# Attention scores of two heads: one matmul over a zero-padded key block, or one matmul per head on half of TensorE's rows

## The chip, the cores and the metric

The kernel runs on one core of one Trainium2 chip. The metric is the device time of one execution in microseconds. Three executions of the kernel before took 631.2, 630.66 and 631.3 us; their median is 631.2 us.

## What is computed

Attention with pooled keys and values, then a channel mix. The shapes are batch 8, 8 heads, 576 positions, head size 64, model width 512, hidden width 1024, all in float32.

```python
k_p = k.reshape(B, H, Sp, pool, D).mean(axis=3)      # 8 positions -> 1: 72 keys
v_p = v.reshape(B, H, Sp, pool, D).mean(axis=3)
scores = scale * np.matmul(q, k_p.transpose(0, 1, 3, 2))
attn = softmax(scores)                               # over the 72 keys
x = (attn @ v_p), heads side by side                 # 4608 positions x 512
xk = mu_k * x + (1.0 - mu_k) * x_prev                # x_prev: the position before
xr = mu_r * x + (1.0 - mu_r) * x_prev
k = np.maximum(xk @ w_k, 0.0)
out = sigmoid(xr @ w_r) * (k * k @ w_v)
```

## The kernel before

The 4608 positions (8 batches of 576) are cut into 36 tiles of 128, and the tiles into chunks of 128, 256 and then eleven times 384 positions. A batch is four and a half tiles long, so tiles 4, 13, 22 and 31 hold the end of one batch and the start of the next, 64 positions each. They are called two-part tiles here; the other tiles have one part.

For each tile the kernel makes scores (`part`, line 719), a softmax over the 72 keys (lines 753 to 796), transposes of the probabilities (`transposed`, line 833, and `transposed_rest`, lines 878 and 888), and for each chunk the product with the values (`attended`, line 931), the mix with the position before (`joined`, line 985), and the three large products of the channel mix: `hidden` (line 1029), `gate` (line 1078) and `mixed` (line 1111). From the third chunk on these large products have float32r operands, split into a high and a low part, three matmuls for each product.

**The scores before.** Heads are taken in four pairs. The query tile `qs` holds a pair's two heads on its 128 partitions: the 64 elements of the first head on partitions 0 to 63, those of the second on 64 to 127. The keys of a batch lie in `kbd` (two of them, for even and odd batches), for each pair 128 partitions by 144 columns: columns 0 to 71 hold the first head's keys on partitions 0 to 63, columns 72 to 143 the second head's on partitions 64 to 127, and the other two quarters are zeros, cleared once. One float32 matmul of 128 rows, 128 weight columns (the queries) and 144 moving columns (the keys) thus gives the scores of both heads (line 729). A tile takes four of them, and a two-part tile eight, each with 64 of the queries as weights. TensorE runs a float32 matmul of this kernel as two passes, each with a weight load of its own, so the profile shows 8 records of matmuls for a tile and 16 for a two-part tile. The scores of pairs 0 and 1 go to the first PSUM bank of `sc`, those of pairs 2 and 3 to the second.

**The softmax.** VectorE takes the maximum of each head's 72 scores (line 753) and subtracts it (line 770, from `sc` to `e`), ScalarE takes the exponential (line 776), VectorE sums (line 778) and inverts (lines 781, 785), and GpSimd or VectorE multiplies (lines 791, 796). There is one `sc`, so the next tile's scores wait for line 770 of this one.

**What sets the order.** Every step is a Python generator with a due time. The class `Order` simulates the engines with a table of durations and writes the instructions of all five engines in the order that its simulation gives. For the scores of a tile it reckons with 1.0 us of TensorE (1.14 for a two-part tile); the change leaves these two figures as they are.

Of the kernel before, what the change touches and what calls it, by code (L numbers as in the profile page):

```python
# [12 lines left out]
ALU = mybir.AluOpType  # L13
AX = mybir.AxisListType
PSUM = bass.MemoryType.PSUM

P = 128
B, H, S, D = 8, 8, 576, 64
POOL = 8
KEYS = S // POOL  # L20
KM = 64
KR = KEYS - KM
NPAIR = H // 2
# [35 lines left out]
LOW_BY = {"k": "gvgvvvgv", "r": "gvgv", "v": "gvvggvgv"}  # L59
BY_HEAD = ((0, 1),)  # L60

BESIDE = (1,)
SQUARED_ON_ACT = (8, 0)
COPIES_ON_ACT = ()
# [166 lines left out]
def dve(n, lock=True):  # L231
    return "dve", 0.067 + n / 960, lock


def act(n, func=None):
    return "act", 0.1 + n / 1200, False, func
# [11 lines left out]
def attention_then_channel_mix(  # L248
# [13 lines left out]
    nc = tc.nc  # L262
# [26 lines left out]
    kbd = [const.tile([P, NPAIR, 2 * KEYS], F32, name=f"kbd{i}") for i in range(2)]  # L289
# [61 lines left out]
    for tag, n in EARLY:  # L351
        t = sb.tile([P, n, 2 * POOL * KEYS], F32, name=f"early_{tag}", tag=tag)
# [16 lines left out]
    def stretches(at, n):  # L369
        o, parts = 0, []  # L370
        while o < n:
            b, s = divmod(at + o, S)
            k = min(S - s, n - o)
            parts.append((b, s, k, o))
            o += k
        return parts

    units = [stretches(a, n) for a, n in zip(starts, CHUNKS)]
    tiles = [
        (c, o, stretches(a + o, P)) for c, (a, n) in enumerate(zip(starts, CHUNKS)) for o in range(0, n, P)  # L380
    ]
# [194 lines left out]
    def sums(st, cols, eng):  # L576

        raw, v = st
        if eng == "t":
            bank, o = yield from summed(v, cols)  # L580
            done_with("stage", raw)
            return "mm", bank, o
        for n in (4, 2, 1):
            yield (dve if eng == "v" else pool)(2 * n * cols)
            halve(nc.vector if eng == "v" else nc.gpsimd, v, cols, n)
        return "stage", raw, v[:, :, :cols]
# [29 lines left out]
    def values(b, p):  # L616
# [3 lines left out]
        if not b:  # L620
            yield need(*[("scored", i) for i in BESIDE])
        kind, raw, o = yield from sums(held.pop(("v", 2 * b + p)), D, SUM_BY.get(f"v{2 * b + p}", "g"))
# [66 lines left out]
    def softmax(i):  # L689

        parts = tiles[i][2]
        if i:
            yield need(("scoring", i - 1))
        yield need(("q", i), *[("keys", b, p) for b, *_ in parts for p in range(1 if i in HALVED else 2)])
        pair = None
        if i in BESIDE:
            pair = [(yield take("mm")), (yield take("mm"))]
            sc = None
            halves = [t.rearrange("p (a n) -> p a n", a=1) for t in pair]
        else:  # L700
            sc = yield take("sc")
            halves = [sc[:, a:a + 1] for a in range(2)]
        held["halves", i] = sc, pair, halves
        if i in HALVED:
            for kind in ("mx", "e", "sm", "px", "pm"):
                held[kind, i] = yield take(kind)
        order.make(("scoring", i))
        if i in HALVED:
            yield from part(i, 0, 1)
        else:  # L710
            yield from part(i, 0, 2)

    def shared(kind, i):
        if (kind, i) not in held:
            held[kind, i] = yield take(kind)
        return held[kind, i]

    def part(i, a0, a1):
        parts, na = tiles[i][2], a1 - a0
        mine = slice(a0, a1)  # L720
        yield need(("scoring", i))
        sc, pair, halves = held["halves", i]
        yield need(*[("keys", b, p) for b, *_ in parts for p in range(a0, a1)])
        qs = held["q", i]
        yield "pe", (1.0 if len(parts) == 1 else 1.14) * na / 2, False
        for g in range(2 * a0, 2 * a1):
            k = (g % 2) * 2 * KEYS
            for b, _, n, o in parts:
                nc.tensor.matmul(  # L729
                    out=halves[g // 2][o:o + n, 0, k:k + 2 * KEYS],  # L730
                    lhsT=qs[:, g, o:o + n], rhs=kbd[b % 2][:, g, :], start=True, stop=True,
                )
        order.make(("scores", i, a0))

        def emptied():
            order.make(("emptied", i, a0))
            if pair:
                for a in range(a0, a1):
                    order.give("mm", pair[a])

        if na == 1:
            svs = [halves[a0]]
        else:
            svs = [sc] if pair is None else halves
        svs = [t[:, :, :4 * KEYS].rearrange("p a (h k) -> p a h k", k=KEYS) for t in svs]
        n = 8 * KEYS // 2 * na
        mx = (yield from shared("mx", i))
        e = (yield from shared("e", i))
        sm = (yield from shared("sm", i))
        at = [mine] if len(svs) == 1 else [slice(0, 1), slice(1, 2)]  # L750
        for sv, o in zip(svs, at):
            yield dve(n // len(svs), False)
            nc.vector.tensor_reduce(out=mx[:, o], in_=sv, axis=AX.X, op=ALU.max)
        if (i, a0) in BY_HEAD:
            yield "dve", 0.11, True
            nc.vector.tensor_scalar(
                out=mx[:, mine], in0=mx[:, mine], scalar1=-scale, scalar2=None, op0=ALU.mult
            )
            yield "act", 1.2 * na, False, "exp"
            for a in range(a0, a1):  # L760
                for h in range(4):
                    nc.scalar.activation(
                        out=e[:, a, h], in_=halves[a][:, 0, h * KEYS:(h + 1) * KEYS], func=AF.Exp, scale=scale,
                        bias=mx[:, a, h], accum_out=sm[:, a, h],
                    )
            emptied()
        else:
            for sv, o in zip(svs, at):
                yield dve(n // len(svs), False)
                nc.vector.tensor_tensor(  # L770
                    out=e[:, o], in0=sv, in1=mx[:, o].broadcast_to([P, (2 if na == 2 and len(svs) == 1 else 1), 4, KEYS]),
                    op=ALU.subtract,
                )
            emptied()
            yield act(n, "exp")
            nc.scalar.activation(out=e[:, mine], in_=e[:, mine], func=AF.Exp, scale=scale)  # L776
            yield dve(n, False)
            nc.vector.tensor_reduce(out=sm[:, mine], in_=e[:, mine], axis=AX.X, op=ALU.add)
        order.make(("maxima", i, a0))
        yield "dve", 0.12, True  # L780
        nc.vector.tensor_scalar(
            out=sm[:, mine], in0=sm[:, mine], scalar1=1e-9, scalar2=float(POOL), op0=ALU.add, op1=ALU.mult
        )
        yield "dve", 0.195, False
        nc.vector.reciprocal(out=sm[:, mine], in_=sm[:, mine])  # L785
        px = (yield from shared("px", i))
        pm = (yield from shared("pm", i))
        v = NORM_BY.get(i, "g") == "v"
        eng = nc.vector if v else nc.gpsimd
        yield dve(4 * KR * na) if v else ("pool", 0.12 + 0.06 * na, True)  # L790
        eng.tensor_tensor(  # L791
            out=px[:, mine], in0=e[:, mine, :, KM:], in1=sm[:, mine].broadcast_to([P, na, 4, KR]), op=ALU.mult
        )
        order.make(("px", i, a0))
        yield dve(4 * KM * na) if v else ("pool", 0.05 + 0.47 * na, True)
        eng.tensor_tensor(
            out=pm[:, mine], in0=e[:, mine, :, :KM], in1=sm[:, mine].broadcast_to([P, na, 4, KM]), op=ALU.mult
        )
        order.make(("pm", i, a0))
# [353 lines left out]
    for i in range(NT):  # L1153
        spare = SPARE if tiles[i][0] > 1 else 0.0
        order.add(tile_due[i], softmax(i), spare)
        order.add(tile_due[i], gathered(i))
        if i in HALVED:
            order.add(tile_due[i] + 0.05, part(i, 1, 2), spare)
        order.add(tile_due[i] + 0.1, transposed(i), spare)
        order.add(tile_due[i] + 0.1, transposed_rest(i), spare)  # L1160
# [63 lines left out]
```

## Time and profile before

| | |
|---|---|
| median of three runs | 631.2 us (630.66 to 631.3) |
| the profiled execution | 631.48 us, of which the profile's span is 629.7 us |
| TensorE matmuls | busy 622.3 us, 99% of the span, 3355 records |
| TensorE weight loads | busy 548.0 us, 87% |
| VectorE, ScalarE, GpSimd | 63%, 56%, 34% |
| granted TensorE clock | 1.0 of full speed |

The profile is one execution. PE is TensorE's matmul row and PEld its weight loads, which run beside matmuls; DVE is VectorE, ACT ScalarE, POOL GpSimd, SP SyncE, which issues the loads and stores. A matmul's record is longer than the time that it holds the array, since matmuls are pipelined: what one costs is read from the distance between the starts of neighbours. A timeline row gives the start and length in microseconds of a run of like instructions and their number (x8); 128*64 means 128 rows and 64 weight columns, 128x144 the partitions and moving columns of the result's rows. Idle time and what ended it stand in brackets.

### The profile page before, as it was taken

What the parts mean: (1) busy time and instruction counts of PE and PEld (TensorE: products, weight loads), DVE (VectorE), ACT (ScalarE), POOL (GpSimd) and SP (SyncE); (2) the same over time, 40 slices, a digit from 0 to 9 for tenths busy, and PEclk for the clock granted to TensorE, in tenths of its full rate; (3) what the DMA queues carried; (4) which work ended last, traced back from release to release, by engine and by line L of the source; (5) the groups of instructions that cost most, each with busy time, mean ns of one, the idle gap of its engine ahead of it and who ended that gap; (6) DMA issues with size and microseconds to landing.
All of it is one profiled execution on the core that took longest, in us unless ns stands there. A gap on an engine that the chain in (4) does not pass through costs nothing.

```text
span 629.7 us, 9238 instructions
## 1 busy us (share of the span) xinstructions
PE 622.3 (99%) x3355; PEld 548.0 (87%) x3355; DVE 394.2 (63%) x792; ACT 350.9 (56%) x755; POOL 215.3 (34%) x338
## 2 busy tenths in 40 slices
PE   8999999999999999999999999999999999999997
PEld 8986559988989989989988988988988988988986
DVE  5999969968824645937635665759854655553411
ACT  3776866766525855556645555545655556454320
POOL 1422287448015128128125019217415106104000
PEclk9999999999999999999999999999999999999999
DMA  8696332051330012411011051032100100000001
GB/s 309 233 364 217 108 128 89 18 179 52 125 110 34 0 34 82 137 34 51 0 34 52 25 193 45 6 137 78 55 34 34 33 18 35 17 1 18 33 1 50
DMA packets 19005, 50.45 MB, mean 80 GB/s; under 512 B 2256, under 2 KB 2512, under 8 KB 18960
## 3 DMA queue, kind: packets, MB, share of 16 engines
q1 hardware_dynamic: 18960, 49.87, 22.6%
q8 instruction: 26, 0.43, 0.3%
q14 instruction: 19, 0.16, 0.1%
HBM read 40.43 MB, written 9.44 MB: 79 GB/s over the span
## 4 chain that ended last, share of the span: by engine, by line
PE 88%; ACT 3%; DVE 3%; POOL 3%; DMA 2%; issue 1%; SPq 0%; POOLq 0%; ACTq 0%; DVEq 0%
PE mm L1029 30%; PE mm L1111 29%; PE mm L1078 16%; PE bank L931 5%; PE sc L729 4%; PE bank L833 2%; DMA got_wr<-in_w_r 1%; DMA stage<-in_kT 1%; PE bank L424 1%; PE bank L434 1%; PE bank L888 1%; POOL stage L559 1%; ACT e L776 0%; ACT tmp L522 0%; DVE got_wk L527 0%
## 5 line engine op out<-in xcount | busy, mean ns | idle before, releaser
L1029 PE MATMUL mm<-xkh,w_k 128*128 128x384 f32 x704 | 180.9, 337 | 0.0
L1111 PE MATMUL mm<-w_v,sh 128*128 128x512 f32 x528 | 173.3, 394 | 0.0
L1029 PEld LDWEIGHTS mm<-xkh,w_k 128*128 128x128 f32 x704 | 126.0, 188 | 1.0 <-issue 0.6
L1029 PE MATMUL mm<-xkl,w_k 128*128 128x384 f32 x352 | 117.7, 335 | 0.0
L1111 PEld LDWEIGHTS mm<-w_v,sh 128*128 128x128 f32 x528 | 99.3, 188 | 19.4
L1111 PE MATMUL mm<-w_v,sl 128*128 128x512 f32 x264 | 103.0, 390 | 0.0
L791 POOL TENSOR_TENSOR px<-e,sm 128x64 f32<-128x64 f32 (+1 forms) x33 | 10.9, 331 | 225.7 <-DVE sm L785 219.9
L1078 PE MATMUL mm<-w_r,xrh 128*128 128x512 f32 x264 | 86.0, 397 | 0.0
L985 DVE SCALAR_TENSOR_TENSOR xm<-bank,given,t 128x384 f32<-128x384 f32 x88 | 50.6, 612 | 40.2 <-POOL t L959 23.0
L944 ACT ACTIVATE t<-bank,om_sb 128x384 f32<-128x384 f32 (+1 forms) x96 | 47.9, 573 | 50.0 <-PE bank L931 49.8
L1052 ACT CAST sh<-rk 128x384 fp32r<-128x384 f32 x88 | 45.0, 513 | 50.2 <-DVE rk L1046 50.0
L1121 DVE TENSOR_TENSOR rs<-mm,rs 128x512 f32<-128x512 f32 x36 | 24.8, 689 | 70.9 <-PE mm L1111 70.7
L1054 DVE TENSOR_TENSOR sl<-rk,sh 128x384 fp32r<-128x384 f32 x88 | 51.9, 592 | 24.8 <-ACT sh L1052 24.4
L1029 PEld LDWEIGHTS mm<-xkl,w_k 128*128 128x128 f32 x352 | 66.1, 188 | 0.0
L1046 DVE SCALAR_TENSOR_TENSOR rk<-mm,rk 128x384 f32<-128x384 f32 x88 | 48.6, 553 | 17.4 <-ACT rk L1039 17.0
L1078 PEld LDWEIGHTS mm<-w_r,xrh 128*128 128x128 f32 x264 | 49.6, 188 | 10.2
L1003 POOL TENSOR_TENSOR xkl<-xm,xkh 128x384 fp32r<-128x384 f32 x44 | 44.7, 1017 | 37.2 <-ACT xkh L1001 37.1
L1111 PEld LDWEIGHTS mm<-w_v,sl 128*128 128x128 f32 x264 | 49.7, 188 | 8.7
L559 POOL TENSOR_TENSOR stage<-stage 128x512 f32<-128x512 f32 (+7 forms) x59 | 51.3, 878 | 13.7 <-DVE w_k L552 11.4
L1039 ACT ACTIVATE rk<-mm 128x384 f32<-128x384 f32 x88 | 43.0, 489 | 20.9 <-PE mm L1029 19.9
L1078 PE MATMUL mm<-w_r,xrl 128*128 128x512 f32 x132 | 51.4, 389 | 0.0
L1003 POOL TENSOR_TENSOR xrl<-xm,xrh 128x384 fp32r<-128x384 f32 x44 | 44.8, 1019 | 1.3 <-ACT xrh L1001 1.2
(144 smaller groups left out, 972.8 us busy)
## 6 DMA issues: line engine op xcount, KB each, us to landing
qs<-in_qT SPq DMA_DIRECT2D x36, 256.0 KB, 3.5
out<-rs SPq DMA_DIRECT2D x36, 256.0 KB, 2.0
stage<-in_kT SPq DMA_DIRECT2D x15, 576.0 KB, 3.8
stage<-in_vm SPq DMA_DIRECT2D x15, 512.0 KB, 4.5
got_wk<-in_w_k SPq DMA_DIRECT2D x8, 512.0 KB, 6.8
got_wv<-in_w_v SPq DMA_DIRECT2D x8, 512.0 KB, 7.5
stage<-in_vr SPq DMA_DIRECT2D x6, 384.0 KB, 4.1
got_wr<-in_w_r SPq DMA_DIRECT2D x4, 512.0 KB, 8.0
```

The source lines that it names most:

```text
L559: nc_eng.tensor_tensor(out=st[:, :, :w], in0=st[:, :, :w], in1=st[:, :, w:2 * w], op=ALU.add)
L931: nc.tensor.matmul(out=xp[:, o], lhsT=v, rhs=p, start=(q == 0), stop=(q == len(terms) - 1))
L944: nc.scalar.activation(out=ts[m][:, 1:n + 1], in_=xp, func=AF.Copy, scale=om_sb[:, m, g:g + 1])
L985: nc.vector.scalar_tensor_tensor(out=xm[:, :n], in0=bank[:, :n], scalar=mu_sb[:, m, g:g + 1], in1=ts, op0=ALU.mult, op1=ALU.add,)
L1003: nc.gpsimd.tensor_tensor(out=lo, in0=xm[:, :n], in1=hi, op=ALU.subtract)
L1029: nc.tensor.matmul(out=hp, lhsT=w[:, o], rhs=x[:, ct, :n], start=(ct == 0 and k == 0), stop=(ct == NCT - 1 and k == len(terms) - 1),)
L1039: nc.scalar.activation(out=rk[:, :n], in_=hp, func=AF.Relu)
L1046: nc.vector.scalar_tensor_tensor(out=rk[:, :n], in0=hp, scalar=0.0, in1=rk[:, :n], op0=ALU.max, op1=ALU.mult)
L1052: nc.scalar.copy(out=sh[:, :n], in_=rk[:, :n])
L1054: nc.vector.tensor_tensor(out=operand("sl", c)[:, jt, :n], in0=rk[:, :n], in1=sh[:, :n], op=ALU.subtract)
L1078: nc.tensor.matmul(out=bank, lhsT=x[:, ct, o], rhs=w, start=(ct == 0 and k == 0), stop=(ct == NCT - 1 and k == len(terms) - 1),)
L1111: nc.tensor.matmul(out=bank, lhsT=s[:, o], rhs=w, start=(jt == 0 and k == 0), stop=(jt == NJT - 1 and k == len(terms) - 1),)
```

## The change

From tile 3 on (`ROWS_FROM = 3`, counted from 0) each matmul of line 729 becomes two: one with the first head's 64 rows of queries and 72 columns of keys, on TensorE's rows 0 to 63, and one with the second head's on rows 64 to 127. The zero quarters of `kbd` are not read. The first head of every pair goes to the first PSUM bank of `sc`, the second head to the second bank. The built program gives these matmuls an array shape of 64 rows by 128 columns (64 by 64 in the two-part tiles), where a one-part tile's had 128 by 128 and a two-part tile's 128 by 64.

```diff
+ROWS_FROM = 3
...
-        parts, na = tiles[i][2], a1 - a0
+        parts, na, rows = tiles[i][2], a1 - a0, i >= ROWS_FROM
...
-        for g in range(2 * a0, 2 * a1):
+        if rows:
+            for g in range(NPAIR):
+                for b, _, n, o in parts:
+                    for a in range(2):
+                        r, k = slice(a * D, (a + 1) * D), g * KEYS
+                        nc.tensor.matmul(
+                            out=halves[a][o:o + n, 0, k:k + KEYS],
+                            lhsT=qs[r, g, o:o + n], rhs=kbd[b % 2][r, g, a * KEYS:(a + 1) * KEYS],
+                            start=True, stop=True,
+                        )
+        for g in range(2 * a0, 2 * a1) if not rows else ():
...
+        by_bank = lambda t: t.rearrange("p a (g r) k -> p r (a g) k", r=2) if rows else t
...
-            nc.vector.tensor_reduce(out=mx[:, o], in_=sv, axis=AX.X, op=ALU.max)
+            nc.vector.tensor_reduce(out=by_bank(mx)[:, o], in_=sv, axis=AX.X, op=ALU.max)
...
-                    out=e[:, o], in0=sv, in1=mx[:, o].broadcast_to([P, (2 if na == 2 and len(svs) == 1 else 1), 4, KEYS]),
+                    out=by_bank(e)[:, o], in0=sv, in1=by_bank(mx)[:, o].broadcast_to([P, (2 if na == 2 and len(svs) == 1 else 1), 4, KEYS]),
```

`e` and `mx` keep their layout by pairs, so what follows line 770 is as before. The order of the instructions is the same on all five engines; in 33 tiles the rows of the scores and of the two VectorE instructions that follow them have another form. The code is twelve lines longer from there on, so that lines 729, 753, 770, 1029, 1078 and 1111 are 732, 765, 782, 1041, 1090 and 1123 in the kernel after.

On TensorE, around a one-part tile between `hidden` and `gate`, before:

```order
L1029 MATMUL mm_119<-xkh_2899,w_k_809 128x384 x2
L1029 MATMUL mm_119<-xkl_2900,w_k_809 128x384
L729 MATMUL sc_113<-kbd_69,qs_105 128x144 x4
L1078 MATMUL mm_118<-w_r_825,xrh_2908 128x512
L1078 MATMUL mm_118<-w_r_825,xrl_2909 128x512
```

And after, at the same place:

```order
L1041 MATMUL mm_119<-xkh_2983,w_k_833 128x384 x2
L1041 MATMUL mm_119<-xkl_2984,w_k_833 128x384
L732 MATMUL sc_113<-kbd_69,qs_105 128x72 x8
L1090 MATMUL mm_118<-w_r_849,xrh_2992 128x512
L1090 MATMUL mm_118<-w_r_849,xrl_2993 128x512
```

Four matmuls of 144 columns have become eight of 72, in the same place between the same neighbours; the first and second of each two stand for rows 0 to 63 and 64 to 127.

On TensorE, around a two-part tile between the last transpose of another tile and `hidden`, before (`kbd_68` and `kbd_69` are the keys of the two batches):

```order
L888 MATMUL bank_114<-ident,pr_94 128x128
L729 MATMUL sc_113<-kbd_68,qs_103 64x144
L729 MATMUL sc_113<-kbd_69,qs_103 64x144
L729 MATMUL sc_113<-kbd_68,qs_103 64x144
L729 MATMUL sc_113<-kbd_69,qs_103 64x144
```

And after:

```order
L900 MATMUL bank_114<-ident,pr_94 128x128
L732 MATMUL sc_113<-kbd_68,qs_103 64x72 x2
L732 MATMUL sc_113<-kbd_69,qs_103 64x72 x2
L732 MATMUL sc_113<-kbd_68,qs_103 64x72 x2
L732 MATMUL sc_113<-kbd_69,qs_103 64x72 x2
```

Each matmul of 64 positions and two heads has become two of one head; the two batches still take turns.

## The prediction

> **What bounds the kernel now.** I read the page first. Its rows give the span, the engines' busy time, TensorE's share and clock in 40 slices, and the chain that ended last.
>
> ```profile
> span 629.7 us, 9238 instructions
> PE 622.3 (99%) x3355; PEld 548.0 (87%) x3355; DVE 394.2 (63%) x792; ACT 350.9 (56%) x755; POOL 215.3 (34%) x338
> PE   8999999999999999999999999999999999999997
> PEclk9999999999999999999999999999999999999999
> PE 88%; ACT 3%; DVE 3%; POOL 3%; DMA 2%; issue 1%; SPq 0%; POOLq 0%; ACTq 0%; DVEq 0%
> ```
>
> TensorE is busy in every slice, at full clock, and it is 88% of the chain. So a microsecond that the scores take from TensorE or give back is a microsecond of the kernel, nearly everywhere. Second, the groups of TensorE by shape, for the scores:
>
> ```profile
> L729 PE MATMUL sc<-kbd,qs 128*128 128x144 f32 x248 | 35.7, 286 | 0.5 <-ACT e L762 0.5
> L729 PE MATMUL sc<-kbd,qs 128*64 128x144 f32 x64 | 4.8, 292 | 0.0
> ```
>
> A record lasts 286 ns, but records overlap. What a tile costs is read third, from the timeline of TensorE around one-part tile 14:
>
> ```profile
> 161.57 0.33 PE L1029 MATMUL mm<-xkl,w_k 128*128 128x384 f32 x1
> 161.74 1.14 PE L729 MATMUL sc<-kbd,qs 128*128 128x144 f32 x8
> 162.63 0.60 PE L1029 MATMUL mm<-xkh,w_k 128*128 128x384 f32 x2
> 163.07 0.34 PE L1029 MATMUL mm<-xkl,w_k 128*128 128x384 f32 x1
> ```
>
> Eight passes span 1.14 us, so they start (1.14 - 0.29) / 7 = 0.122 us apart, and the tile holds TensorE for 8 x 0.122 = 0.98 us. The change reaches tiles 3 to 35: four two-part tiles (4, 13, 22, 31) and 29 one-part tiles, some 28 us of TensorE for the latter. That is all there is to win or to multiply.
>
> **Part one: the pace of a pass.** The new passes have half the moving columns, 72 for 144, hence half of 0.122 us: 0.06. But each still loads 128 weight columns. What a load of 128 columns allows is seen where the moving side is short:
>
> ```profile
> 86.46 0.27 PE L931 MATMUL bank<-pth,vbd_l 128*128 128x192 f32 x1
> 86.57 0.28 PE L931 MATMUL bank<-ptl,vbd_h 128*128 128x192 f32 x1
> 86.68 0.27 PE L931 MATMUL bank<-ptr,vbd_r 96*128 96x192 f32 x1
> 86.79 0.28 PE L931 MATMUL bank<-pth,vbd_h 128*128 128x192 f32 x1
> ```
>
> These float32r passes of 192 columns start 0.11 us apart, though line 1029's of 384 columns start 0.17 us apart (161.57 to 161.74), so that 192 would need about 0.085. The weight load sets 0.11. So a new pass takes 0.11 us and not 0.06, if it doesn't wait for the load of the other head's half.
>
> **Part two: do two halves run side by side?** There are now 16 passes for a one-part tile. One after the other they would take 16 x 0.11 = 1.76 us, in twos 8 x 0.11 = 0.88. No row of before has 64 rows. The nearest is a two-part tile, where two matmuls of 64 weight columns use the two halves of the array's columns. Tile 13, matmuls and weight loads, then the loads' durations by shape, and the first hundredths of its block in a narrow window:
>
> ```profile
> 147.47 0.39 PE L1111 MATMUL mm<-w_v,sl 128*128 128x512 f32 x1
> 147.70 0.40 PE L1111 MATMUL mm<-w_v,sh 128*128 128x512 f32 x1
> 148.03 1.20 PE L729 MATMUL sc<-kbd,qs 128*64 128x144 f32 x16
> 149.16 0.62 PE L1029 MATMUL mm<-xkh,w_k 128*128 128x384 f32 x2
> 149.61 0.34 PE L1029 MATMUL mm<-xkl,w_k 128*128 128x384 f32 x1
> ```
>
> ```profile
> 148.02 0.93 PEld L729 LDWEIGHTS sc<-kbd,qs 128*64 128x64 f32 x16 [0.37 <-issue]
> 149.16 0.30 PEld L1029 LDWEIGHTS mm<-xkh,w_k 128*128 128x128 f32 x2 [0.20 <-issue]
> ```
>
> ```profile
> L729 PEld LDWEIGHTS sc<-kbd,qs 128*128 128x128 f32 x248 | 33.6, 190 | 3.1 <-issue 1.4 <-ACT e L762 0.7
> L729 PEld LDWEIGHTS sc<-kbd,qs 128*64 128x64 f32 x64 | 3.7, 136 | 1.3 <-issue 1.3
> ```
>
> ```profile
> 148.02 0.14 PEld L729 LDWEIGHTS sc<-kbd,qs 128*64 128x64 f32 x2 [0.37 <-issue]
> ```
>
> Sixteen passes of 144 columns span 1.20 us, where sixteen in a row would take 16 x 0.122 = 1.95: they run in twos, 7 x 0.122 + 0.29 = 1.14 plus 0.06 at the start. Two loads lie within 0.14 us, about one load's 136 ns: loads run in twos as well. I take the same for row halves: eight steps of 0.11. A bound on the other side is 0.122, the step of the column halves.
>
> **Part three: the price of another array shape.** The same block shows what it costs to leave the 128x128 shape and return. Between like matmuls of line 1111 the step is 147.70 - 147.47 = 0.23 us, but 0.33 into the block: +0.10. From the block's first matmul to the third of line 1029 it is 149.61 - 148.03 = 1.58 us, where the one-part tile needs 163.07 - 161.74 = 1.33 for the same eight steps: +0.25. Together 0.35 us a block. The weight-load row has the cause in brackets: PEld sat idle 0.37 us before the block and 0.20 us after it, where loads otherwise run ahead under the matmuls. The two-part tiles pay this already; after the change the 29 one-part tiles have another shape than their neighbours too. The Trainium skill, "TensorEngine Tiling (Array Packing)", section Key Properties, says that changing the tiling mode drains TensorE, whichever the mode; the column halves here agree with 0.35 us, and no run shown has row halves. Below, the price would be nothing if row halves need no drain: the 96-row matmul above stands among 128-row ones at 0.11 us without a gap. I take 0.35, from the row that has a changed shape, and zero makes a rival.
>
> **The sum for a one-part tile.** The first load is exposed: 64 columns in the price above, 128 now. The load records differ by 190 - 136 = 54 ns, so +0.05. The streaming from the first load's end: 8 x 0.122 = 0.98 before, 7 x 0.11 + 0.06 = 0.83 now, -0.15. In all 0.35 + 0.05 - 0.15 = +0.25 us, and 29 x 0.25 = +7.25 us.
>
> **The two-part tiles** keep their price and go from eight steps of two to eight steps of four passes (row and column halves). The step lies between 0.06 (72 columns, and a load of 64) and 0.122 (nothing gained); midway it saves 8 x 0.03 = 0.25 us. Tile 4's saving is worth nothing, since TensorE waits for VectorE behind it:
>
> ```profile
> 38.87 1.20 PE L729 MATMUL sc<-kbd,qs 128*64 128x144 f32 x16
> 40.54 0.70 PE L1029 MATMUL mm<-xkh,got_wk 128*128 128x256 f32 x2 [0.47 <-DVE xkh L985]
> ```
>
> So 3 x 0.25 = -0.75 us.
>
> **VectorE** gets the same elements in another order: 72 in a row are still neighbours.
>
> ```profile
> L770 DVE TENSOR_TENSOR e<-sc,mx 128x576 f32<-128x576 f32 x34 | 25.6, 754 | 0.9
> L753 DVE TENSOR_REDUCE mx<-sc 128x8 f32<-128x576 f32 x34 | 25.5, 751 | 26.7 <-PE sc L729 26.6
> ```
>
> I cost it at nothing. Line 753 waits 26.7 us in all for TensorE's scores, so this softmax starts when it is told to, and VectorE is idle for 37% of the span. Even 0.2 us more in each would be 33 x 0.4 = 13 us of that idle time. Scores that come a quarter of a microsecond later are hidden in the same way: TensorE, busy 99% of the span, hardly ever waits for a softmax now. No DMA, no wait and no instruction order changes.
>
> Sum: 7.25 - 0.75 = +6.5 us on the profiled 631.48, so 638.0; that execution is 0.28 above the median, and from the median 631.2 it is **637.7 us**. About 0.2%, 1.3 us, can be told from no change.
>
> **The forecast's own bounds.** The price of the shape may be 0.25 to 0.40, the step 0.10 to 0.122: a one-part tile from 0.25 + 0.05 - (0.98 - 0.76) = +0.08 to 0.40 + 0.05 - 0.07 = +0.38, or +2.3 to +11.0 us, the two-part tiles 0 to -1.5. Both ends at once are unlikely: 633.5 to 642.
>
> **Rival one: no price for row halves (faster).** If loads run ahead as before, a one-part tile goes from 0.98 to 0.88 us: 29 x -0.10 - 0.75 = -3.65 us, 627.5. It decides as soon as a block's two ends, first load included, cost less than the 0.15 us that the streaming gains plus 0.75 / 29 = 0.03, so 0.18 in place of 0.40. For it: the 96-row matmuls. Against it: the idle weight loader on both sides of tile 13's block. If the load didn't pace the passes either, 8 x 0.06 = 0.49 would remain, 29 x -0.49 - 1.5 = -15.7 us, 615.5; the 0.11 us of the 192-column passes excludes that for me. The same skill page, section Theoretical Speedup, allows up to 2x for a contraction of 64 or less, which is that far end. I give rival one 0.16 and its far end 0.01.
>
> **Rival two: the halves' loads queue.** If row halves load one after the other, a tile streams 15 x 0.11 + 0.06 = 1.71 us: 0.35 + 0.05 + 1.71 - 0.98 = +1.13, times 29 = +32.8 us, 664. Against it: the loads of column halves in twos. Chance 0.07.
>
> **Rival three: a half's load waits for that half's matmul.** Then a step is 0.11 + 0.06 = 0.17: 0.40 + 7 x 0.17 + 0.06 - 0.98 = +0.67, times 29 = +19.4 us, 650.6. Against it: in the one-part tile before, a step is 0.122 and not 0.11 + 0.122, so loads run under matmuls on the same rows. The Trainium skill, "TensorE: Matmul & The Clock Gate", section The mechanism, has a load overlap matmuls in flight only where the row group differs; by that rule it would be this rival, and those steps disagree with it. Chance 0.08.
>
> **How the numbers follow.** The forecast has the remaining 0.68. Rival one and the forecast hold 0.84, less some tail beyond either: the range is 627 to 643. Slower is the forecast but for a sliver, and rivals two and three: 0.78. Faster is rival one and that sliver's end: 0.18. Within 0.2%: 0.04.
>
> **What would show it.** In the profile after, a one-part tile's 16 passes of 72 columns should span about 0.83 us from the first start to the last plus a record; line 732's weight loads should show idle time before them in 33 blocks, as should the loads behind; from the block's first matmul to the third of the next group should be about 1.48 us. Blocks without idle loads around them prove rival one; a block of 1.7 us, rival two; 1.25 us, rival three. VectorE's lines 765 and 782 should stay near 0.75 us. If TensorE's time outside the blocks moves, the whole sum is wrong.

## The result and the profile after

The kernel after takes 637.67 us (median of four runs, 637.08 to 638.32), the kernel before 631.25 us in the same comparison: a ratio of 1.0102, with a 95% interval of 1.009 to 1.0115. It is slower by 6.4 us; the forecast was 637.7 us, +6.5.

The page of the kernel after, against the same rows of before: TensorE is busy 6.9 us longer, in 296 records more, and every other engine is as it was.

```profile
span 636.5 us, 9831 instructions
PE 629.2 (99%) x3651; PEld 545.8 (86%) x3651; DVE 393.3 (62%) x792; ACT 350.6 (55%) x755; POOL 215.3 (34%) x338
PE 90%; DMA 2%; DVE 2%; ACT 2%; POOL 1%; issue 1%; SPq 0%; DVEq 0%; ACTq 0%
```

The block of one-part tile 14 in the kernel after, first TensorE's matmuls, then its weight loads, then the first 0.01 us of the block in a narrow window:

```profile
163.91 0.34 PE L1041 MATMUL mm<-xkl,w_k 128*128 128x384 f32 x1
164.18 1.11 PE L732 MATMUL sc<-kbd,qs 64*128 64x72 f32 x16
165.23 0.62 PE L1041 MATMUL mm<-xkh,w_k 128*128 128x384 f32 x2
165.69 0.33 PE L1041 MATMUL mm<-xkl,w_k 128*128 128x384 f32 x1
```

```profile
164.18 0.97 PEld L732 LDWEIGHTS sc<-kbd,qs 64*128 64x128 f32 x16 [0.25 <-issue]
165.22 0.30 PEld L1041 LDWEIGHTS mm<-xkh,w_k 128*128 128x128 f32 x2
```

```profile
164.18 0.33 PE L732 MATMUL sc<-kbd,qs 64*128 64x72 f32 x2
```

Two passes start together, one on each half. Sixteen passes span 1.11 us and one lasts 0.27, so the last starts 0.84 us after the first: seven steps of 0.11 between eight pairs of passes, and 0.05 more in the first, where the load is exposed. Before the block the weight loader is idle for 0.25 us. Behind it the view prints no idle time in brackets, since the gap is only 0.07 us (164.18 + 0.97 = 165.15 to 165.22); in the kernel before, the next load began 0.06 us before the block's last one had ended (161.57 + 1.09 = 162.66 to 162.60):

```profile
161.57 1.09 PEld L729 LDWEIGHTS sc<-kbd,qs 128*128 128x128 f32 x8
162.60 0.31 PEld L1029 LDWEIGHTS mm<-xkh,w_k 128*128 128x128 f32 x2
```

The idle loader that the forecast expected at both ends of a block is thus there: in all 29 one-part tiles the gap ahead is longer than before, and the gap behind is 0.07 us, less than the 0.20 of tile 13 before. The step into the block is 0.27 us (163.91 to 164.18) where it was 0.17, and from the block's first matmul to the third of line 1041 it is 1.51 us where it was 1.33. A one-part tile thus costs 0.10 + 0.18 = +0.28 us.

The block of two-part tile 13, whose sixteen passes have become thirty-two:

```profile
150.83 0.73 PE L732 MATMUL sc<-kbd,qs 64*64 64x72 f32 x32
151.49 0.62 PE L1041 MATMUL mm<-xkh,w_k 128*128 128x384 f32 x2
151.94 0.34 PE L1041 MATMUL mm<-xkl,w_k 128*128 128x384 f32 x1
```

From its first matmul to the third of the next group it is 1.11 us instead of 1.58: -0.47. The step of four passes is (0.73 - 0.23 - 0.05) / 7 = 0.064 us, with 0.23 for one record and 0.05 for the first load.

VectorE's two instructions with the new order, by shape, take what they took, and wait for the scores as they did:

```profile
L782 DVE TENSOR_TENSOR e<-sc,mx 128x576 f32<-128x576 f32 x34 | 25.6, 754 | 0.9
L765 DVE TENSOR_REDUCE mx<-sc 128x8 f32<-128x576 f32 x34 | 25.6, 752 | 26.7 <-PE sc L732 26.1
```

To see where the time came from, take the start of a block in both kernels. Tile 13's moved from 148.03 to 150.83, by 2.80 us. The last one's, tile 35's, in before and in after:

```profile
555.52 1.14 PE L729 MATMUL sc<-kbd,qs 128*128 128x144 f32 x8
```

```profile
562.19 1.12 PE L732 MATMUL sc<-kbd,qs 64*128 64x72 f32 x16
```

It moved by 6.67. Between the two lie 19 one-part and 3 two-part tiles: 19 x 0.28 - 3 x 0.47 = 3.9 us, and 3.87 is what was added. Ahead of tile 13 it is less clean. The scores of tile 0, which the change doesn't touch, already start 0.72 us later in this profile than in that of before:

```profile
10.37 0.69 PE L729 MATMUL sc<-kbd,qs 128*128 128x144 f32 x4
```

```profile
11.09 0.69 PE L740 MATMUL sc<-kbd,qs 128*128 128x144 f32 x4
```

That is the start of the program, which differs from run to run (9.60 to 11.09 us in the nine profiles of this case). From there to tile 13 the kernel after loses 2.80 - 0.72 = 2.1 us. The nine one-part tiles add 9 x 0.27 = 2.4. Tile 4 with the wait for VectorE behind it takes 0.58 us less: from the block's start to line 1041's next matmul it is 41.11 - 40.02 = 1.09 us, where it was 40.54 - 38.87 = 1.67. And a later wait for VectorE, 0.30 us, is new:

```profile
41.11 1.56 PE L1041 MATMUL mm<-xkh,got_wk 128*128 128x256 f32 x6 [0.36 <-DVE xkh L997]
52.02 1.35 PE L1041 MATMUL mm<-xkh,got_wk 128*128 128x256 f32 x5 [0.30 <-DVE sh L1058]
```

Together 2.4 - 0.58 + 0.30 = 2.1. So of the 6.8 us between the two spans about 6.1 are from the blocks and the waits near them, and 0.7 from the start.

### The profile page after: what moved, and what is told of

It is laid out like the page before. It is cut to its first block, busy times and chain, and to the rows that moved or that the text cites. A ratio compares the mean times of both kernels' runs of the same rounds, so it can differ in the third digit from the quotient of the medians.

```text
span 636.5 us, 9831 instructions
## 1 busy us (share of the span) xinstructions
PE 629.2 (99%) x3651; PEld 545.8 (86%) x3651; DVE 393.3 (62%) x792; ACT 350.6 (55%) x755; POOL 215.3 (34%) x338
## 4 chain that ended last, share of the span: by engine, by line
PE 90%; DMA 2%; DVE 2%; ACT 2%; POOL 1%; issue 1%; SPq 0%; DVEq 0%; ACTq 0%
PE mm L1123 32%; PE mm L1041 29%; PE mm L1090 15%; PE bank L943 5%; PE sc L732 5%; PE bank L845 2%; DMA got_wv<-in_w_v 2%; DMA got_wk<-in_w_k 1%; POOL stage L560 1%; PE bank L435 1%; PE bank L425 1%; PE bank L900 1%; ACT tmp L523 1%; PE mm L571 0%; DVE got_wv L528 0%
```

## The experiments

The theory was that of the forecast: a block whose array shape differs from its neighbours' pays for two changes of shape; inside it the halves run side by side, and the load of 128 weight columns sets the pace. Rival A put the loss down to the doubled number of matmuls, rival B to VectorE's reading and writing by bank. Times of before vary from one comparison to the next (631.05 to 631.48), so each ratio is against the runs beside it.

**All 128 rows, everything else as after.**

```diff
-                            lhsT=qs[r, g, o:o + n], rhs=kbd[b % 2][r, g, a * KEYS:(a + 1) * KEYS],
+                            lhsT=qs[:, g, o:o + n], rhs=kbd[b % 2][:, g, a * KEYS:(a + 1) * KEYS],
```

> As the kernel after, with the same sixteen passes of 72 columns, the same banks and the same VectorE instructions, but each matmul takes all 128 rows (the keys' zero quarter is read again), so the array keeps its 128x128 shape and two heads can't run side by side. Theory (two halves in twos, paced by the 128-column load; price of the shape): 16 steps of 0.11 = 1.76 us in place of 0.98, no idle weight loader around the block, 29 x 0.78 = +22.6 us on 631.25, 654 us. Rival A (the after kernel's loss is the doubled number of matmuls, 8 passes more for 0.25 us): the same count, so the same time as after, 637.7. Rival B (the loss is VectorE's reading and writing by bank): 637.7 too.

Measured: 653.84 us, ratio 1.0359 (1.0345 to 1.0374). The block of tile 14:

```profile
167.68 0.33 PE L1041 MATMUL mm<-xkl,w_k 128*128 128x384 f32 x1
167.85 1.90 PE L732 MATMUL sc<-kbd,qs 128*128 128x72 f32 x16
169.55 0.59 PE L1041 MATMUL mm<-xkh,w_k 128*128 128x384 f32 x2
169.99 0.33 PE L1041 MATMUL mm<-xkl,w_k 128*128 128x384 f32 x1
```

The step into the block is 0.17 us again, so no price at its edge, but sixteen passes follow one another at (1.90 - 0.27) / 15 = 0.109 us, though they stream only 72 columns. The load sets the pace, and the row halves of the kernel after do run side by side: without that it would be 16 us slower still. That it is the load, and not some least time of a pass, is seen in this run's tile 13, with all rows and 72 moving columns too, but loads of 64 columns for two column halves:

```profile
154.04 1.27 PE L732 MATMUL sc<-kbd,qs 128*64 128x72 f32 x32
```

Its thirty-two passes run in twos, (1.27 - 0.23 - 0.05) / 15 = 0.066 us a step. Rivals A and B both forecast 637.7 us, and the same number of matmuls with the same banks and VectorE work took another time.

**Row halves in the two-part tiles alone.**

```diff
-        parts, na, rows = tiles[i][2], a1 - a0, i >= ROWS_FROM
+        parts, na, rows = tiles[i][2], a1 - a0, i >= ROWS_FROM and len(tiles[i][2]) > 1
```

> The change in the four two-part tiles alone, which had an array shape of their own already. Theory: no further price; the block behind the first start shrinks from 1.13 to 0.66 us in tiles 13, 22 and 31, and tile 4's gain goes into the wait behind it: 3 x -0.47 = -1.4 us, 629.8. Rival A (number of matmuls): these tiles go from 16 to 32 passes, four times 0.5 us more, 633. Rival B (VectorE): four tiles of 33, no change that can be measured.

Measured: 629.86 us, ratio 0.9979 (0.997 to 0.9988). Where the shape was changed already, row halves are a gain: 1.2 us from three tiles. Tile 4's went into a longer wait, as its row shows (0.80 us for VectorE, where it was 0.47):

```profile
39.28 0.73 PE L732 MATMUL sc<-kbd,qs 64*64 64x72 f32 x32
40.81 1.56 PE L1041 MATMUL mm<-xkh,got_wk 128*128 128x256 f32 x6 [0.80 <-DVE xkh L997]
```

**The price by itself: column halves in the kernel before.**

```diff
-            for b, _, n, o in parts:
+            cut = parts
+            if i >= 3 and len(parts) == 1:
+                cut = [(parts[0][0], 0, 64, 0), (parts[0][0], 0, 64, 64)]
+            for b, _, n, o in cut:
```

> The kernel before, whose one-part tiles from tile 3 on are cut as two-part tiles are: 64 queries on each half of the array's columns, 144 columns of keys with their zeros, same banks and VectorE instructions as before. Streaming is unchanged (eight steps of 0.122), so that this is the price of another shape alone. Theory: 0.35 us x 29 = +10.2 us, 641.4, with the weight loader idle on both sides of each block. Rival A (number of matmuls, 16 passes as in after): +7, 638. Rival B (VectorE by bank): 631.25.

Measured: 640.87 us, ratio 1.0153 (1.0139 to 1.0167), +9.8 us. Tile 14, matmuls and loads:

```profile
164.29 0.34 PE L1032 MATMUL mm<-xkl,w_k 128*128 128x384 f32 x1
164.56 1.20 PE L732 MATMUL sc<-kbd,qs 128*64 128x144 f32 x16
165.69 0.61 PE L1032 MATMUL mm<-xkh,w_k 128*128 128x384 f32 x2
166.14 0.34 PE L1032 MATMUL mm<-xkl,w_k 128*128 128x384 f32 x1
```

```profile
164.56 0.93 PEld L732 LDWEIGHTS sc<-kbd,qs 128*64 128x64 f32 x16 [0.25 <-issue]
165.69 0.30 PEld L1032 LDWEIGHTS mm<-xkh,w_k 128*128 128x128 f32 x2 [0.20 <-issue]
```

The work is that of before, no wait was added, and the weight loader now stands idle 0.25 us ahead of the block and 0.20 us behind it: 0.10 + (1.58 - 1.33) = 0.35 us, 29 times 10.2. The price belongs to the shape: the 638 us of rival A and the 631.25 of rival B lie outside the interval (631.05 x 1.0139 = 639.8 to 641.6).

**Four quarters everywhere.**

```diff
+            cut = parts if len(parts) > 1 else [(parts[0][0], 0, 64, 0), (parts[0][0], 0, 64, 64)]
             for g in range(NPAIR):
-                for b, _, n, o in parts:
+                for b, _, n, o in cut:
```

> The kernel after, whose one-part tiles are cut at 64 queries too, so that from tile 3 on all scores use the four quarters of the array, 64 rows by 64 columns, four passes side by side. Theory: the price of the shape stays (0.10 before, 0.02 behind), the block goes to the 0.66 us that the two-part tiles show in after, against 0.885: 29 x (0.66 + 0.11 - 0.885) = -3.3 us and -1.4 from the two-part tiles: 626.5, faster than before. Rival A (number of matmuls, 32 passes for 8): 29 x 0.75 = +22 us, 653. Rival B (VectorE by bank): as after, 637.7.

Measured: 626.61 us, ratio 0.9931 (0.9917 to 0.9944). This version beats both kernels, by 4.4 us and by 11. Tile 14:

```profile
159.64 0.34 PE L1042 MATMUL mm<-xkl,w_k 128*128 128x384 f32 x1
159.91 0.73 PE L733 MATMUL sc<-kbd,qs 64*64 64x72 f32 x32
160.57 0.62 PE L1042 MATMUL mm<-xkh,w_k 128*128 128x384 f32 x2
161.03 0.34 PE L1042 MATMUL mm<-xkl,w_k 128*128 128x384 f32 x1
```

The entry costs what it costs in the kernel after (0.27 us into the block), but the load is now of 64 columns, and the step falls from 0.11 to 0.064 us. The tile takes 0.10 + 1.12 - 1.33 = -0.11 us, so that the streaming gain at last exceeds the price: 29 x -0.11 - 1.4 = -4.6. Rivals A (653) and B (637.7) fall.

**A change of shape inside the block.**

```diff
-                        r, k = slice(a * D, (a + 1) * D), g * KEYS
+                        r, k = slice(0, P) if g == 2 else slice(a * D, (a + 1) * D), g * KEYS
```

> As the kernel after, but the third of the four pairs is computed with all 128 rows (the same 72 columns, banks and semaphores, the zero quarter read again), so that a one-part tile's block goes row halves, full rows, row halves, with no wait between. Theory (the price is the change of shape, at any place): the third pair takes four passes of 0.11 for two steps, +0.22, and there is one more round trip at 0.42 us (0.27 net in the kernel after plus the 0.15 that its streaming saves): 29 x 0.64 = +18.6, the two-part tiles +2, 658 us. Rival (the idle weight loader belongs to the start and end of a tile's scores, to their semaphores, and is paid once): +0.22 x 29 and +0.5, 644.5 us.

Measured: 652.08 us, ratio 1.0324 (1.0309 to 1.0339). The direction is the theory's, the size is not. The block spans 1.64 us where it spanned 1.11:

```profile
166.55 1.64 PE L732 MATMUL sc<-kbd,qs 64*128 64x72 f32 x16
```

That is +0.53 and not +0.64; less 0.22 for the two added steps, two changes cost 0.31 us, some 0.15 each. I had taken the price at the block's edge as it stood. If the last pass before any change needs only its streaming (0.06 us) and not a load's time (0.11), each change gives back 0.05, and 0.42 - 2 x 0.05 = 0.32 would remain; that fits the 0.31, but no run isolates it. 29 x 0.53 and the two-part tiles' 1.3 make 654.3; 2 us of that are missing. They are not missing from the later blocks: from tile 13's start to tile 35's it is 422.5 us (152.77 to 575.29) where it was 411.4 (150.83 to 562.19), +11.2, and 19 x 0.52 + 3 x 0.44 for the two-part tiles make 11.2. What is missing lies earlier. Nothing ahead of tile 3 is changed, yet its block starts at 27.75 us in the profile of after and at 26.43 here, which is the start of the program. Between tiles 3 and 13 this kernel loses 3.3 us to the one after where the blocks add 9 x 0.52 + 0.44 = 5.1; the two waits for VectorE of the kernel after, 0.36 us at 41.11 and 0.30 at 52.02, don't stand in this trace, and the rest of that gap is open. The rival (paid once, 644.5) falls: with no semaphore between, the change still costs.

**The same matmuls with the heads apart.**

```diff
-            for g in range(NPAIR):
-                for b, _, n, o in parts:
-                    for a in range(2):
+            for a in range(2):
+                for g in range(NPAIR):
+                    for b, _, n, o in parts:
```

> The very matmuls of the kernel after in another order: all four pairs' first heads, then all second heads, so that neighbours lie on the same row half (in the two-part tiles the two column halves still take turns). Theory (TensorE starts matmuls in the program's order, and two passes run side by side only where neighbours use different halves): a one-part tile streams 16 steps of 0.11 but for one overlap, 15 x 0.11 + 0.06 = 1.71 against 0.83, 29 x 0.88 = +25.5; two-part tiles 16 steps of 0.06 for 8: +0.5 x 3; in all 664.7 us. Rival (each half has a queue of its own that runs ahead): 637.7 us.

Measured: 651.48 us, ratio 1.0312 (1.0295 to 1.0329). Neither side was right. The block spans 1.62 us, 12 steps, not 16 and not 8:

```profile
167.17 1.62 PE L732 MATMUL sc<-kbd,qs 64*128 64x72 f32 x16
```

Where the halves overlap is seen in windows of tile 14's block, which count the records in flight (the first PE and PEld columns with their counts):

```profile
167.16:167.60 0.44, 0.43 (x4) 0.43 (x4) 0.00 (x0) 0.00 (x0) 1.00 0.00 0
167.67:168.00 0.33, 0.33 (x8) 0.33 (x8) 0.00 (x0) 0.00 (x0) 1.00 0.00 0
```

In the kernel after, the first 0.44 us of tile 14's block hold twice as many:

```profile
164.18:164.62 0.44, 0.44 (x8) 0.44 (x8) 0.00 (x0) 0.00 (x0) 1.00 0.00 0
```

So with the heads apart the first half runs alone for half a microsecond, and then the second half joins it. Two windows over the loads, up to 167.67 and up to 167.68 us, show when:

```profile
167.16 0.63 PEld L732 LDWEIGHTS sc<-kbd,qs 64*128 64x128 f32 x5 [0.25 <-issue]
167.16 0.69 PEld L732 LDWEIGHTS sc<-kbd,qs 64*128 64x128 f32 x6 [0.25 <-issue]
```

The records don't name the half. But the sixth load comes 0.51 us into the block and 0.07 us after the fifth, where the loads of one half are 0.11 apart, so I take it for the second half's first: the first half's fifth pass has then started, and three of its passes, with their loads, still wait. The second half starts ahead of them, so the order of starts is not strictly the program's; but it doesn't look further ahead than that. A strict order was my premise and fell. The Trainium skill, "TensorE: Matmul & The Clock Gate", section The mechanism, says that matmuls start in strict order and are never reordered; this trace disagrees where they lie on different row halves.

**The heads in twos**, to test that reading.

```diff
-            for g in range(NPAIR):
+            for g, a in [(g + d, a) for g in (0, 2) for a in range(2) for d in range(2)]:
                 for b, _, n, o in parts:
-                    for a in range(2):
+                    if True:
```

> Between the kernel after and the one with the heads apart: pairs 0 and 1 of the first heads, then of the second heads, then pairs 2 and 3 in the same way, so that two matmuls (four passes) on the same row half stand in a row. Theory, formed on the run with the heads apart (TensorE starts passes of the other half ahead of earlier ones that still wait, if no more than some three passes with their loads stand before them): the second half starts a pass or so late and then keeps up, one step of 0.11 more in a one-part tile, 29 x 0.11 = +3 us on the kernel after, 641 us. Rival (strict program order; the heads apart ran side by side for another reason): four passes of the first half, then three side by side at most in each change of half, about five steps more, 29 x 0.56 = +16, 654 us.

Measured: 640.58 us, ratio 1.014 (1.0121 to 1.0159). Four passes on one half before the other's turn cost next to nothing: the block spans 1.17 us for 1.11.

```profile
166.96 1.17 PE L732 MATMUL sc<-kbd,qs 64*128 64x72 f32 x16
```

Two loads start within the first 0.02 us, though three more passes of the first half stand ahead of the second half's first:

```profile
166.96 0.20 PEld L732 LDWEIGHTS sc<-kbd,qs 64*128 64x128 f32 x2 [0.25 <-issue]
```

The added 0.06 is half of the step that I gave it; 29 x 0.06 = 1.7 us would make 639.4, within the interval (631.3 x 1.0121 = 638.9 to 641.3). That the median came so near to the 641 is luck, then. The profiled execution, at 641.99 the longest of the four, also has an early wait for VectorE of 1.77 us, where the kernel after has 0.30; why it is longer is not shown.

```profile
54.55 1.78 PE L1041 MATMUL mm<-xkh,got_wk 128*128 128x256 f32 x7 [1.77 <-DVE sh L1058]
```

Strict order (654 us) falls again.

## Why the prediction was right, point by point

- **TensorE carries the time.** Right from tile 13 to tile 35, where what the blocks added is what the program lost, 3.9 us by the count and 3.87 by the starts. Ahead of tile 13 the waits for VectorE changed too, and 0.72 us lie ahead of anything that the change touches.
- **The pace of a pass.** Right: 0.11 us, set by the load of 128 weight columns, in the kernel after for two side by side and with all rows for one at a time. Rival three (a half's load waits for that half's matmul, 0.17 a step) would have given a row of 0.05 + 7 x 0.17 + 0.27 = 1.5 us and is excluded by the 1.11 us of the block's row.
- **Two halves side by side.** Right, taken from the column halves of the two-part tiles and shown by two starts together at 164.18, and by the all-rows run, 16 us slower with the same matmuls. This excludes rival two.
- **The price of another shape.** Right: 0.35 us a block by the column-half run, and row halves pay the same 0.10 us at the entry; with the exit a tile costs +0.28, where the sum had +0.25. This excludes rival one: the 96-row matmul that spoke for it stands among 128-row ones without a gap, but row halves do not. The Trainium skill, "TensorEngine Tiling (Array Packing)", section Key Properties, says that a change of mode drains the engine; the three shapes here agree, in that the loads don't run ahead and each entry costs 0.10 us more, and the runs give the size: 0.15 us net for a change inside a block, or about 0.20 by estimate, if the last pass gives back 0.05.
- **The sum for a one-part tile.** +0.25 was forecast, +0.28 measured (0.27 by single records, averaged over the tiles): 29 x 0.27 = 7.9 for 7.25.
- **The two-part tiles** were the mis-sized term. I took the middle of 0.06 and 0.122 for the step of four passes; it is 0.064, near the lower bound, so that a tile saves 0.47 us and not 0.25, and three of them 1.4 us and not 0.75. Tile 4's gain went into a longer wait in the run with the two-part tiles alone, as forecast; in the kernel after it didn't, for the wait behind it is 0.36 us where it was 0.47, and only 0.30 us of it was lost, to the later wait. The two errors, +0.65 and -0.65, cancel: 7.9 - 1.4 = 6.5. That the total came out to 0.1 us is in large part luck: tile 4 is a third error, of 0.3 us, and the start of the program alone differs by more than a microsecond from run to run.
- **VectorE at nothing.** Right: 754 and 752 ns an instruction, as before.

## What to carry to other kernels

Using part of the array for small matmuls pays a price at the block's edges (here 0.35 us for leaving the full shape and coming back; weight loads didn't run ahead across the change), so count what the block streams: here matmuls on half of the array saved about 0.13 us of a 0.98 us block and lost (a price of 0.40 with the exposed first load, +0.27 in all), and matmuls on a quarter, whose loads have half the columns too, saved enough to win. Look at the weight load before the moving side: here, with 128 weight columns, it set a pace of 0.11 us for 72 moving columns that need 0.06. Where a block has already left the full shape, cutting it finer added no price here.

## What was not expected of the hardware

- Four quarters start a pass each within one step of 0.064 us, 16 ns a pass; two halves need 0.11 us a step for two.
- Passes on one row half start ahead of earlier ones on the other half, across three waiting passes, but not across a whole block of eight.
- A change of shape inside a block cost less than the block's edges suggest: two such changes took 0.31 us, not 0.42. That the last pass before a change takes 0.06 us instead of 0.11 would account for it; this is argued from the sum and not shown by itself.
